# Two units' exponentials in one instruction, under a newly searched order table, in a fused RG-LRU and soft-MoE kernel

## The chip, the cores and the metric

The kernel runs on one core of one Trainium2 chip. The metric is the device time of one execution in microseconds (us). The engines are called PE (TensorE), DVE (VectorE), ACT (ScalarE), POOL (GpSimd) and SP (SyncE, which issues all DMAs of this kernel on one in-order queue).

## The reference

A gated linear recurrence over 4 sequences of 5056 tokens with 256 channels, and a soft mixture of 8 experts with 32 slots over its 20224 outputs. All tensors are float32.

```python
a_base = 1 / (1 + exp(-a_param))
sig_r, sig_i = sigmoid(r_gate), sigmoid(i_gate)
a_t = exp(8 * sig_r * log(clip(a_base, 1e-6, 1 - 1e-6)))
x_gated = sqrt(max(1 - a_t * a_t, 1e-6)) * sig_i * x
for t in range(S):                       # per sequence and channel
    h = a_t[:, t] * h + x_gated[:, t]
    y[:, t] = h
logits = y @ phi                         # 20224 x 32
d = softmax of logits over the tokens
slot_input = d.T @ y                     # 32 slots x 256
slot_out[e] = relu(slot_input[e] @ w1[e]) @ w2[e]
out = softmax of logits over the slots @ slot_out
```

## The kernel before

The tokens are cut into 40 blocks of 512 (the last has 256), numbered 0 to 39. Blocks go in units, mostly of two: 0; 1, 2; 3, 4; 5; 6, 7; 8, 9; and so on to 38, 39. A unit is named by its first block. A block passes through these steps, written with the block's number and, where there are two channel halves, the half:

- r, i and x are loaded (three DMAs of 512 KB). PE transposes r to channels by tokens (rp, L397); ACT takes its sigmoid, or tanh of half of it where the exponential table is active (sr, L409). Per unit, ACT takes the sigmoid of i (si, L420, 128x2048 for two blocks).
- Per unit, ACT computes a = exp(...) (ex), one instruction per channel half, since each half has its own scale. After a sigmoid only a scale is needed (L460), after a tanh a scale and a bias too (L462); both are pointers to a 128x1 column.
- POOL computes a*a (sq, L471) and i*x (u, L432). Per unit, ACT takes sqrt(1 - a*a) (qr, L478).
- PE transposes i*x into PSUM (up, L490). DVE multiplies it with the root (st, L500) and runs the scan (sc, L513), one block and half after the other. PE transposes y back (yp, L533); a copy brings each half block to SBUF (yc), on ACT (L286) or DVE (L288).
- Every four blocks, PE makes logits (lp, L579), DVE takes the running maximum (ls, L589 and L592), PE transposes (ep, L603 and L606), ACT takes exponentials (ee, L612, and md, L597, for the rescaling), PE adds up slots by y (acc, L621), DVE keeps the sum (as, L632).

The functions sigmoid, exp and sqrt sit in different ACT tables, so ACT goes round in stretches: it collects the exponentials and then the roots of about three units and pays an ACT_TABLE_LOAD at each switch. In the plan, copies go with any table and tanh with those of exp and sigmoid.

After the last block come the end of the softmax over tokens (mall, L661; mp, L668; mx; mc, L678; wj; we; W), the slot inputs (sp, L696; slot, L699), the experts on PE (hp, L761; ht, L773; so, L788), and the outputs: logits are transposed per group of four blocks (ct, L841), made to weights (c0, cm, c1, c2, c3, L847 to L861), transposed (hc, L865; hx) and multiplied with the experts' result (op, L894), copied (og, L286 or L288) and stored. Some of ct to c3 run while the experts do.

The order of all of this is written out by hand: ORDER is a table of 1247 numbers, each an operation; a "b" behind a number takes its second engine. The class Plan replays the table with costs to place the tiles: all of r, i, x, a, a*a, weights and outputs live in one tile g (called big in the code) of 19 pairs of 128x2x1024. Each engine, SP too, issues in the table's order. EXM is a list of pairs of units whose exponentials are to be one operation; it is empty before. In e_ex two units are put into one instruction per half when both were made by the same function (plain) and their pairs lie near enough for one strided access pattern; else they follow each other.

Of the kernel before, what the change touches and what calls it, by code (L numbers as in the profile page):

```python
# [13 lines left out]
NEG = -1.0e30  # L14
UNITS = [1] + [2] + [2, 1] + [2] * 17
TANH_I = []
EXM = []
LAST = 3
FIRST = (6, 4)
N_PAIR = 19  # L20
# [6 lines left out]


ORDER = """
# [16 lines left out]
322b 532 864 374 863 375 865 360 320 866 391 393 413 394 395 361 398 362 396 414 379 381 613 417 363 399 397 382  # L46
400 434 454 475 495 435 476 488 507 529 651 711 508 670 467 733 530 489 453 432 380b 472 418 415 419 416 634 632
654 439 436 437 440 868 714 633 635 614 513 715 875 473 477 455 656 438 441 458 456 459 457 460 876 480 478 481
479 877 482 867 869 655 870 871 597 872 873 401 420 736 515 421b 737 402b 556 494 535 514 496 442 499 738 879
497 500 498 739 657 878 880 422 423 501 403 404 443 598 516 536 618 557 577 517 874 537 521 461 463 464 444 881  # L50
518 882 883 540 716 884 445b 599 558 538 519 522 520 752 774 549 548 631 653 692 570 630 589 611 652 671 693 571
590 612 554 462b 717 502 885 523 503 673 483 484 485 486 539 504 505 541 524 886 526 527 887 542 555 562 888 563
559 675 755 560 636 674 595 676 677 757 576 581 695 564 561 525 779 637 596 578 890 756 758 889 780 697 698 891
696 600 565 582 579 583 580 658 617 567 638 777 778 568b 720 679 603 892 893 894 895 566 601 604 602 619 622 543
545 605 544 896 623 546 624 620 621 639 659 640 721 741 680 700 753 793 897 606 796 898 660 641 899 672 694 712
713 608 584 644 607b 585b 625 626b 722 627 586 587b 681 642 645 643 661 646 662 993 795 984 815 794 735 817 663
798 901 664 609 665 775 734 754 965 964 816 970 678 969 776 682 685 908 900 902 761 683 686 684 687 961 699 903
904 905 909 628 910 906 704 718 688 647 648b 689b 666 701 800 797 820 705 907 762 706 702 649 818 650b 821 759
819 690 719 723 740 703 912 668 913 799 911 669b 802 724 667 725 742 707 708 726 709 745 760 782 781 914 915 916
917 767 803 823 801 822 763 727 743 728 746 744 918 747 729 731 764 919 748 920 730 768 765 921 710b 749b 691b  # L60
732b 783 750 786 804 751b 769 766 787 1115 923 805 784 808 924 770 772 925 926 927 928 788 806 785 809 807 810
771b 773b 824 1093 789 791 827 790b 828 825 829 826 930 811 931 813 941 942 932 934 812b 814b 935 943 792 950
967 985 972 981 979 968 989 982 988 971 980 977 978 974 983 966 976 987 975 962 992 973 990 991 986 963 830 945
933 946 922 944 936 951 937 938 939 831 1116 952 953 947 948 929 954 955 956 940 949 1071 1017 957 1039 958 999
1072 1117 1018 994 1073 1000b 995b 1019 959 960 1094 1020 1021 1095 1001 1004 996 997 1040 1009 1118 1005 1002
1074 1075 1010b 1006 1007 998 1011 1003 1096 1119 1012 1097 1041 1042 1043 1008 1013 1022 1098 1044 1076 1120
1045 1014 1015 1016b 1077 1078b 1046 1047 1053 1048b 1050b 1049 1051 1057b 1054b 1099 1055 1100 1059 1056b 1060b
1062b 1063b 1181 1065 1067b 1159 1061 1182 1160 1183 1068b 1069b 1066b 1079 1080b 1081b 1083 1082 1161 1023
1024b 1108 1086 1109 1112 1111b 1110b 1025 1087 1162 1163 1089b 1088b 1090b 1225 1121 1026 1029 1226 1227 1164
1027b 1184 1101 1165 1122b 1028b 1102b 1104b 1032 1103 1105 1166b 1033b 1034 1035 1130 1036b 1131b 1174 1203  # L70
1175b 1177b 1178b 1228 1176b 1133 1134 1132 1185 1186 1204 1205 1229 1230 1123 1124 1127b 1187 1126b 1125 1188
1167 1168 1206 1169b 1171b 1170 1207 1052 1058 1064 1070 1231 1189 1190 1137 1191b 1232b 1193b 1192b 1138 1139
1140 1141 1233 1240 1241 1242 1243 1234b 1235b 1236b 1237b 1244b 1196 1197 1200b 1142 1143 1198 1199b 1208 1209
1144 1152 1153 1156 1154b 1145 1146 1210b 1155b 1218 1219 1222 1147 1148 1220b 1221b 1211 1212 1214 1215b 1149b
1213b 1085 1084 1113 1114 1091 1030 1092 1031 1038 1107 1136 1037 1106 1128 1129 1173 1179 1194 1195 1180 1135
1245 1172 1246 1201 1238 1158 1239 1223 1216 1150 1224 1202 1217 1151 1157
"""


# [11 lines left out]
class Plan:  # L91
# [13 lines left out]
    def op(self, key, eng, us, emit, deps=(), alloc=(), uses=(), act=""):  # L105
        o = Op(key, eng, us, emit, list(deps), list(alloc), list(uses), act)
        assert key not in self.by_key, key
        self.ops.append(o)
        self.by_key[key] = o
# [66 lines left out]
def kernel(  # L176
# [78 lines left out]
    def cols(w):  # L255
        return min(C, NTOK - w * C)


    ident = const.tile([P, P], F32, name="ident")
# [19 lines left out]
    op = plan.op  # L279
# [29 lines left out]
    op(("ident",), "POOL", 0.6, e_ident)  # L309
    op(("ap",), "DMA", 1.7, lambda o: nc.sync.dma_start(out=G(("apl",))[:H, :P], in_=a_param.rearrange("(h p) -> h p", p=P)), alloc=[("G", ("apl",))])  # L310
    op(("yones",), "POOL", 0.3, e_ones)
    op(("misc",), "POOL", 3.2, e_misc)
    op(("phi",), "DMA", 0.2, lambda o: nc.sync.dma_start(out=phi_sb, in_=phi.rearrange("(h p) s -> p h s", p=P)))

    def e_apt(o):
# [41 lines left out]
    def window(w):  # L357
# [80 lines left out]

        exu = [u_ for u_ in units if any(u_[0] in m and u0 in m for m in EXM)] or [unit]
        exk = next((m[-1] for m in EXM if u0 in m), u0)  # L440
        exn = sum(cols(v) for u_ in exu for v in u_) / C
# [524 lines left out]
```

## Time and profile before

| | |
|---|---|
| time, median of 3 runs (range) | 303.35 us (302.66 to 303.78) |
| the profiled execution's own time; its span | 302.85 us; 300.9 us |
| busy: PE, DVE, ACT, POOL | 237.1, 241.3, 241.7, 181.9 us |
| moved by DMA | 100.0 MB: 78.9 read, 20.7 written |
| ACT_TABLE_LOADs | 24 of 1.283 us |

An engine's busy time is averaged over very different stretches. Up to about 27 us blocks are loaded and no scan can run; to about 217 us the blocks pass; to about 246 us PE works on the slots and experts; then the output is written. Which engine has no slack is read per stretch. The span leaves out about 2 us that lie around it in the measured time.

### The profile page before, as it was taken

Reading aid. Unit: us, or ns where it says so; the run is one execution under the profiler, and the core shown is the slowest. Engines: PE = TensorE matmul, PEld = TensorE weight load, DVE = VectorE, ACT = ScalarE, POOL = GpSimd, SP = SyncE. Lnnn points to the kernel's source line nnn. Section 1 sums busy time; section 2 is a strip of 40 time slices with the busy share of each in tenths; the row PEclk is TensorE's granted clock in tenths of the full one; section 3 lists DMA queues with packets and bytes.
Section 4 is the critical chain, followed back from the end, with each engine's and each line's share of the span. In section 5 each row is a group of like instructions: output and inputs, shape, how many; then the busy total and the mean of one; then the engine's idle time right before and its main releaser. Section 6 shows DMA issues by size and latency. Waiting matters only on the chain.

```text
span 300.9 us, 5789 instructions
## 1 busy us (share of the span) xinstructions
PE 237.1 (79%) x2140; PEld 165.0 (55%) x2140; DVE 241.3 (80%) x380; ACT 241.7 (80%) x310; POOL 181.9 (60%) x122
## 2 busy tenths in 40 slices
PE   4606789789896988798898978999899999968500
PEld 4505566565774866557556654757463567655300
DVE  1003999899999999999999999989978759997600
ACT  4999999999999999999999999998223048866400
POOL 4489578995899969799479997895001140022000
PEclk9956999999999999799999999999999999999955
DMA  6999999978998969949997799999990029999997
GB/s 260 380 415 409 400 408 410 401 273 286 413 408 334 411 246 318 378 114 376 412 362 278 256 376 374 344 407 372 332 370 6 2 92 380 403 399 407 377 411 293
DMA packets 28032, 100.03 MB, mean 332 GB/s; under 512 B 3362, under 2 KB 3364, under 8 KB 28004
## 3 DMA queue, kind: packets, MB, share of 16 engines
q1 hardware_dynamic: 28004, 99.66, 86.2%
q8 instruction: 17, 0.28, 0.4%
q14 instruction: 11, 0.09, 0.1%
HBM read 78.94 MB, written 20.71 MB: 331 GB/s over the span
## 4 chain that ended last, share of the span: by engine, by line
PE 28%; DVE 25%; ACT 14%; DMA 10%; issue 8%; POOL 8%; SPq 1%; ACTq 0%; DVEq 0%; POOLq 0%
DVE g L513 11%; DMA g<-in_r_gate_dram 8%; DVE b L500 6%; PE b L894 6%; POOL g L471 4%; ACT g L409 4%; PE b L397 4%; ACT g L462 3%; POOL g L432 3%; PE b L579 3%; PE b L533 3%; PE b L490 2%; PE b L761 2%; DVE y L288 2%; PE b L788 2%
## 5 line engine op out<-in xcount | busy, mean ns | idle before, releaser
L432 POOL TENSOR_TENSOR g<-g 128x1024 f32<-128x1024 f32 (+1 forms) x40 | 93.0, 2345 | 21.6 <-ACT g L420 18.0
L513 DVE TENSOR_TENSOR_SCAN g<-g,b 128x512 f32<-128x512 f32 (+4 forms) x86 | 99.1, 1176 | 0.5
L471 POOL TENSOR_TENSOR g<-g 128x1024 f32<-128x1024 f32 (+1 forms) x40 | 73.8, 1871 | 12.0 <-ACT g L462 8.6
L500 DVE SCALAR_TENSOR_TENSOR b<-g,b 128x512 f32<-128x512 f32 (+1 forms) x80 | 51.7, 676 | 25.7 <-ACT g L478 25.2
L490 PE MATMUL b<-ident,g 128*128 128x128 f32 x316 | 48.3, 285 | 20.9 <-POOL g L432 16.1
L397 PE MATMUL b<-ident,g 128*128 128x128 f32 x316 | 47.7, 292 | 9.0 <-DVE g L513 4.2
L490 PEld LDWEIGHTS b<-ident,g 128*128 128x128 f32 x316 | 35.4, 144 | 33.8 <-POOL g L432 22.4
L533 PE MATMUL b<-ident,g 128*128 128x128 f32 x316 | 46.0, 280 | 6.3 <-DVE g L513 4.5
L397 PEld LDWEIGHTS b<-ident,g 128*128 128x128 f32 x316 | 37.4, 149 | 18.8 <-DVE g L513 7.1
L533 PEld LDWEIGHTS b<-ident,g 128*128 128x128 f32 x316 | 34.3, 141 | 20.5 <-DVE g L513 8.1
L861 POOL TENSOR_TENSOR y<-y,rs 128x512 f32<-128x512 f32 x10 | 10.4, 1048 | 57.9 <-DVE rs L858 40.0
L409 ACT ACTIVATE g<-b 128x512 f32<-128x512 f32 (+1 forms) x80 | 43.1, 605 | 2.1 <-PE b L397 2.1
L288 DVE COPY y<-b 128x512 f32<-128x512 f32 x58 | 38.2, 678 | 1.8 <-PE b L533 1.3
L420 ACT ACTIVATE g<-g 128x2048 f32<-128x2048 f32 (+2 forms) x22 | 38.4, 1755 | 0.1
L478 ACT ACTIVATE g<-g 128x2048 f32<-128x2048 f32 (+2 forms) x22 | 37.3, 1737 | 0.1
L462 ACT ACTIVATE g<-g,ca 128x1024 f32<-128x1024 f32 (+2 forms) x32 | 33.8, 1135 | 0.0
L286 ACT COPY g<-b 128x512 f32<-128x512 f32 (+1 forms) x51 | 24.3, 548 | 10.6 <-PE b L894 10.3
L894 PE MATMUL b<-soR,y 32*128 32x256 f32 x320 | 26.9, 402 | 2.2 <-DVE y L288 0.6
L288 DVE COPY g<-b 128x512 f32<-128x512 f32 (+1 forms) x37 | 22.2, 648 | 3.5 <-PE b L894 3.2
L621 PE MATMUL b<-y,e 128*32 128x257 f32 x316 | 22.4, 385 | 0.6 <-ACT e L612 0.4
L894 PEld LDWEIGHTS b<-soR,y 32*128 32x128 f32 x320 | 18.4, 184 | 7.9 <-ACT g L286 2.6
L286 ACT COPY y<-b 128x512 f32<-128x512 f32 x31 | 17.5, 589 | 6.3 <-PE b L533 6.3
(86 smaller groups left out, 233.8 us busy)
## 6 DMA issues: line engine op xcount, KB each, us to landing
g<-in_x_dram SPq DMA_DIRECT2D x39, 512.0 KB, 7.3
g<-in_i_gate_dram SPq DMA_DIRECT2D x39, 512.0 KB, 7.9
out_dram<-g SPq DMA_DIRECT2D x39, 512.0 KB, 5.7
g<-in_r_gate_dram SPq DMA_DIRECT2D x38, 512.0 KB, 6.5
g<-in_moe_w_dram SPq DMA_DIRECT2D x32, 512.0 KB, 6.2
g<-in_r_gate_dram SPq DMA_DIRECT2D x3, 256.0 KB, 5.5
g<-in_x_dram SPq DMA_DIRECT2D x1, 256.0 KB, 4.6
g<-in_i_gate_dram SPq DMA_DIRECT2D x1, 256.0 KB, 6.4
```

The lines of the kernel that those rows point to most:

```text
L286: nc.scalar.copy(out=dst, in_=srct)
L288: nc.vector.tensor_copy(out=dst, in_=srct)
L397: nc.tensor.transpose(out=by_tile(rp, n)[:, j, :], in_=rows(("r", w), n)[:, j, h * P : (h + 1) * P], identity=ident,)
L409: nc.scalar.activation(halves(("A", w))[:, h, :c], Bk(("rp", w, h))[:, :c], f, scale=k)
L432: nc.gpsimd.tensor_tensor(out=rows(("x", w), n), in0=rows(("i", w), n), in1=rows(("x", w), n), op=ALU.mult)
L462: nc.scalar.activation(a, a, AF.Exp, scale=ca[:, h : h + 1], bias=ca[:, h : h + 1])
L471: nc.gpsimd.tensor_tensor(out=halves(("N", w))[:, :, :c], in0=a, in1=a, op=ALU.mult)
L490: nc.tensor.transpose(out=by_tile(up, n)[:, j, :], in_=rows(("x", w), n)[:, j, h * P : (h + 1) * P], identity=ident,)
L500: nc.vector.scalar_tensor_tensor(up, halves(("N", w))[:, h, :c], 5e-4 if twice else 1e-3, up, op0=ALU.max, op1=ALU.mult)
L513: nc.vector.tensor_tensor_scan(dst, dst, up[:, s0:s1], init, op0=ALU.mult, op1=ALU.add)
L533: nc.tensor.transpose(out=yp[:, j, h * P : (h + 1) * P], in_=halves(("A", w))[:, h, (2 * i + j) * P : (2 * i + j + 1) * P], identity=ident,)
L894: nc.tensor.matmul(Bk(("op",) + tag + (n,))[:, i * D : (i + 1) * D], hT()[r, (2 * i2 + i) * P : (2 * i2 + i + 1) * P], soR[r, :], start=Tr ...
```

## The change

Four pairs of units are named in EXM: 12 and 14, 18 and 20, 30 and 34, 36 and 38. ORDER is another table throughout. The fixed setup operation misc is planned to follow ident.

```diff
-EXM = []
+EXM = [(12, 14), (18, 20), (30, 34), (36, 38)]
 ORDER = """
-1 74 96 5 115 2 0 3 6 7 8 9 10 77 79 101 99 118 78 102 80 100 119 120 83 121 11 16 14 15 33 55 36 58 124 17 60
+5 1 33 55 11 115 74 96 116 34 13 56 12 75 97 138 35 137 57 178 200 76 159 98 219 241 160 179 201 117 0 3 6 7 8 9
...
-    op(("misc",), "POOL", 3.2, e_misc)
+    op(("misc",), "POOL", 3.2, e_misc, deps=[("ident",)])
```

In the built program, the pairs 12 and 14, 30 and 34, 36 and 38 become two instructions of 128x2x2x512 each. Units 18 and 20 stay in four instructions: 18 is made by sigmoid and 20 by tanh in the new order. For unit 38 the new access pattern takes both blocks whole, the last 256 columns of block 39 too, which hold nothing that is read later. ACT has 36 exponentials of blocks instead of 44: 6 of L460 (12 before), 20 of L462 with two blocks (24 before), 4 with one whole block (6 before), none with 256 columns (2 before), and the 6 new ones. Of the 79 copies of y (yc), ACT makes 29 (25 before) and DVE 50 (54 before). There are 24 ACT_TABLE_LOADs before and after, 80 st, 86 scan instructions, and the same DMAs in another order. On DVE, between the first st of unit 30 and that of unit 36, there stand 2 copies of y and 1 as (5 and 2 before); as_7 now stands between the st and the sc of block 38.

On ACT, the exponentials of units 12 and 14, first before, then after. Before, those of 14 (L460) come two sr behind those of 12.

```order
L462 ACT_TABLE_LOAD
L462 ACTIVATE g<-g,ca 128x2x512 x2
L409 ACTIVATE g<-b_76 128x512
L409 ACTIVATE g<-b_70 128x512
L460 ACTIVATE g<-g,ca_91 128x2x512 x2
```

```order
L462 ACT_TABLE_LOAD
L462 ACTIVATE g<-g,ca 128x2x2x512 x2
L409 ACTIVATE g<-b_73 128x512
L597 ACTIVATE d_127<-m_104,n_116 128x1
L612 ACTIVATE e_68<-b_77 128x512
L409 ACTIVATE g<-b_72 128x512
L462 ACTIVATE g<-g,ca 128x2x512 x2
```

Afterwards one double instruction per half covers both, and 14 is among those with a bias. The last row is unit 16.

On ACT, the way to qr_36 and what follows it, before and after. L462 is ex_38 before (with ex_36 and si_38, L420, further ahead), L478 128x2048 is qr_36, L478 128x1024 and 128x2x256 are qr_38, and the L286 are copies of y.

```order
L462 ACTIVATE g<-g,ca 128x512
L462 ACTIVATE g<-g,ca 128x256
L462 ACTIVATE g<-g,ca 128x512
L462 ACTIVATE g<-g,ca 128x256
L478 ACT_TABLE_LOAD
L478 ACTIVATE g<-g 128x2048
L286 COPY y_65<-b_77 128x2x256
L286 COPY y_64<-b_70 128x2x256
L286 COPY y_62<-b_75 128x2x256
L286 COPY y_63<-b_73 128x2x256
L478 ACTIVATE g<-g 128x1024
L478 ACTIVATE g<-g 128x2x256
```

```order
L597 ACTIVATE d_132<-m_109,n_121 128x1
L286 COPY y_66<-b_74 128x2x256
L286 COPY y_63<-b_73 128x2x256
L286 COPY y_62<-b_71 128x2x256
L286 COPY y_66<-b_72 128x2x256
L478 ACT_TABLE_LOAD
L478 ACTIVATE g<-g 128x2048
L478 ACTIVATE g<-g 128x1024
L478 ACTIVATE g<-g 128x2x256
L420 ACT_TABLE_LOAD
L420 ACTIVATE g<-g 128x1024
L420 ACTIVATE g<-g 128x512
```

Afterwards the exponentials of 36 and 38 stand further ahead, in one pair of instructions, four more copies of y stand between qr_30 and qr_36, none stands between qr_36 and qr_38, and si_38 with a table load of its own (the last three rows) has moved behind qr_38.

On PE, from the last copy of y's transposes to the first acc of the last group, before and after: L533 is yp, L603 and L606 are ep_10, L668 is mp, which needs the last maximum of DVE.

```order
L533 MATMUL b_73<-ident,g 128x128 x4
L603 MATMUL b_75<-ident,n_125 128x32
L606 MATMUL b_75<-ident,l_87 128x32
L603 MATMUL b_75<-ident,n_125 128x32
L606 MATMUL b_75<-ident,l_87 128x32
L621 MATMUL b_71<-y_67,e_68 32x257
L621 MATMUL b_71<-y_63,e_68 32x257
L621 MATMUL b_71<-y_64,e_68 32x257
L668 MATMUL b_77<-ident,m_113 1x128
```

```order
L533 MATMUL b_73<-ident,g 128x128 x4
L668 MATMUL b_77<-ident,m_113 1x128
L533 MATMUL b_71<-ident,g 128x128 x4
L603 MATMUL b_74<-ident,n_125 128x32
L606 MATMUL b_74<-ident,l_87 128x32
L603 MATMUL b_74<-ident,n_125 128x32
L606 MATMUL b_74<-ident,l_87 128x32
L621 MATMUL b_73<-y_66,e_69 32x257
```

Before, ep_10 and three acc stand ahead of mp; afterwards mp comes first, and a yp, ep_10 and all of acc_9 and acc_10 stand behind it. Between the last acc and the first hp, PE has three ct, sp and a fourth ct (two ct, sp and a third ct before); the ct that is new there comes from the output part.

More of the change, by code (lines that the diff above doesn't have):

```diff
@@ L29 @@
 ORDER = """
[16 rows of a table removed]
[L46 to L75, printed above, removed]
@@ L76 @@
-1245 1172 1246 1201 1238 1158 1239 1223 1216 1150 1224 1202 1217 1151 1157
[15 rows of a table added]
+507 431 592 508 529 299b 852 530 531 532 611 613 612 614 472 858 509 510 318 354 376 373 355 377 391 411 432 452
+473 392 493 320 337 359 339 319 321 859 374 361 340 360 362 338 465 487 424 464 627 486 446 648 730 415 378 380
+393 412 381 396 860 861 733 653 397 413 398 862 394 416 430 711 587 609 505 527 506 528 451 379b 433 474 470 395
+417 414 492 471 713 630 631 654 712 714 511 864 865 437 456 871 872 438 457 439 453 434 632 478 873 458 435 454
@@ new lines @@
+436 479 455 866 735 867 875 868 475 595 633 736 513 734 876 863 869 418 399 401 459 461 419b 402b 460b 554 476
+480 477 651 420 497 870 400 462 498 421 512 533 516 481 519 483 482 499 494 596 514 534 616 652 874 555 575 515
+597 556 495 484 496 877 878 879 538 880 520 440 441 517 442 535 882 536 518 521 443 539 540 537 881 522 667 500
+883 670 502 668 588 610 628 546 689 568 975 672 649 789 811 547 569 552 553 690 629 650 989 749 770 523b 634 671
+593 541 574 503 884 501 557 560 816 561 543 562 558 544 886 792 542b 673 674 692 576 693 559 594 885 793 887 598
@@ new lines @@
+579 601 635 615 655 752 888 889 890 753 580 602 581 577 603 599 578 775 694 794 620 891 621 600 622 717 776 817
+814 795 695 773 774 815 617 563 565 566 676 618 892 619 604 582 893 584 583 894 524 638 636 656 637 718 738 677
+697 585 895 606 657 641 605b 525b 607b 564b 719 678 660 754 623 897 625 639 658 642 640 710 709 731 669 732 691
+790 812 963 986 965 750 771 969 985 751 772 643 661 659 662 675 715 696 682 679 904 905 626 680 683 906 716 756
+898 755 737 757 701 908 698 681 684 699 702 700 703 723 720 899 900 739 901 902 624b 798 685 686b 663 664b 909
@@ new lines @@
+704 644 705b 665 687 646 896 645b 666b 688b 647b 758 778 759 721 724 722 725 740 799 819 800 742 743 741 903 910
+760 911 706 912 707 744 915 913 763 916 726 745 777 779 782 761 764 762 796 747 917 919 765 780 783 781 784 746b
+727b 748b 766 768 728 1089 767b 920 918 729b 978 977 966 791 971 813 979 962 987 983 968 959 957 797 801 804 921
+818 820 922 923 924 823 805 802 907 769b 914 803 806 974 972 961 824 821 825 822 982 981 958 988 960 967 976 973
+964 980 984 970 785 1067 926 927 786b 807 928 787 937 938 808b 929 788 930 939 946 931 826 827b 940 947 809 810b
@@ new lines @@
+941 932 933 942 948 949 943 934 944 935 1090 950 1068 925 951 945 936 952 1013 1111 1035 953 1177 954 1091 990
+1112 1113 1000 1114 991b 1036 1014 1037 1038 1039 995 992 996 1005 1001 997 1002 993 1069 1015 1070 1115 1016
+1006 1092 998 1071 1017 994 1003 999 1007 1008 1004 1009 1178 1093 1179 1010 955 1116 1040 1018 1094 1072 1041
+956 1011 1073 1042 1074 1180 1012b 1055 1056 1057 1059b 1058b 1043 1049 1044 1047 1050 1053 1046b 1045b 1061
+1095 1052b 1065b 1096b 1062b 1063b 1051 1181 1064 1075 1076b 1077b 1079 1078 1082 1199 1019 1083b 1086b 1084b
@@ new lines @@
+1085 1200 1020 1201 1182 1104 1155 1105b 1107 1156 1097 1157 1133 1108b 1202 1106b 1098b 1099b 1028 1029b 1032b
+1031b 1117 1101 1100 1134 1135 1030 1118b 1021 1022b 1024b 1136 1158 1119 1221 1183 1120b 1184b 1122b 1123b 1025
+1023 1121 1159 1160 1126 1161 1127b 1162b 1129b 1128b 1222 1223 1130 1137 1185 1186 1203 1170 1189b 1187b 1188b
+1138 1192 1171 1174b 1173b 1224 1172b 1193 1204 1196 1139 1163 1140b 1194b 1195b 1148 1164 1167 1165 1225 1149
+1150 1205 1226 1151b 1152b 1166 1206b 1214 1215 1218 1217 1216b 1060 1048 1054 1066 1227 1228b 1141 1207 1208b
@@ L77 @@
+1209b 1210b 1142 1143 1145 1211 1144 1229 1236 1230 1231 1237 1240 1233 1239 1238b 1232b 1080 1081 1087 1088
+1110 1103 1109 1033 1102 1034 1026 1124 1027 1125 1131 1132 1175 1191 1190 1176 1153 1197 1168 1220 1219 1147
+1213 1198 1242 1234 1235 1146 1154 1212 1169 1241
 """
```

29 rows, old and new, of the table ORDER are left out of this document.

## The prediction

> **What bounds the kernel now.** I read the stretches first: the span cut where the first root of units 0, 6, 12, 18, 24, 30 and 36 reaches DVE, then where the experts and the output begin. Columns: stretch, length, busy time of PE, PEld, DVE, ACT, POOL, clock, DMA.
>
> ```profile
> 0.00:26.90 26.90, 9.53 (x57) 8.73 (x58) 0.95 (x6) 22.83 (x30) 17.08 (x38) 0.78 0.92 361
> 26.90:59.20 32.30, 26.33 (x206) 20.52 (x204) 30.07 (x39) 32.21 (x36) 26.41 (x14) 0.97 1.03 406
> ...
> 145.90:175.50 29.60, 26.52 (x228) 17.96 (x224) 28.91 (x44) 29.51 (x30) 23.40 (x12) 1.00 0.86 320
> 175.50:203.00 27.50, 24.37 (x217) 15.52 (x216) 26.14 (x34) 27.38 (x34) 24.41 (x13) 1.00 0.98 377
> 203.00:225.10 22.10, 20.51 (x185) 13.34 (x188) 20.09 (x38) 10.03 (x20) 4.07 (x3) 1.00 0.99 365
> 225.10:246.40 21.30, 21.16 (x255) 10.96 (x254) 15.74 (x43) 6.03 (x13) 5.16 (x5) 1.00 0.02 5
> 246.40:300.90 54.50, 32.27 (x352) 23.06 (x344) 33.54 (x62) 27.27 (x56) 5.19 (x5) 0.85 0.97 381
> ```
>
> From 27 to 203 us ACT never rests and DVE hardly does. At 203 ACT becomes free (10 of 22.1 us) while DVE and PE go on; then PE alone works, then DMA writes. The waits say who leads in the long part:
>
> ```profile
> DVE b L500 <- ACT g L478: 25.2, 5, 22.9
> ACT y L286 <- PE b L533: 6.3, 3, 2.7
> ...
> 173.88 0.72 DVE L589 TENSOR_SCALAR_CACHE_REDUCE l<-b,m 128x512 f32<-128x512 f32 x1
> 175.45 1.29 DVE L500 SCALAR_TENSOR_TENSOR b<-g,b 128x512 f32<-128x512 f32 x2 [0.59 <-ACT g L478]
> 203.01 1.29 DVE L500 SCALAR_TENSOR_TENSOR b<-g,b 128x512 f32<-128x512 f32 x2 [1.30 <-ACT g L478]
> ```
>
> DVE (L500 is st) waits for a root (L478) five times, 22.9 us of it at the start; the other four are 2.3 us together, 1.30 of them for qr_36. ACT waits for transposes of y (L533) three times, and the first row shows that there is no place for that before 203. So ACT paces the blocks through its roots, and DVE, filled up with copies of y, arrives just ahead of each: both are full, but a lighter DVE alone would only wait longer. A saving counts if it brings qr_36 forward and DVE has no more to do before it than ACT; after qr_36, DVE and PE set the end of the blocks, and DMA that of the kernel.
>
> **ACT up to qr_36.** Its rows:
>
> ```profile
> L420 ACT ACTIVATE g<-g 128x2048 f32<-128x2048 f32 x18 | 34.8, 1931 | 0.1
> L462 ACT ACTIVATE g<-g,ca 128x1024 f32<-128x1024 f32 x24 | 28.4, 1252 | 0.0
> L460 ACT ACTIVATE g<-g,ca 128x1024 f32<-128x1024 f32 x12 | 12.9, 1145 | 0.0
> L420 ACT ACT_TABLE_LOAD x7 | 9.0, 1283 | 0.1
> L420 ACT ACTIVATE g<-g 128x1024 f32<-128x1024 f32 x3 | 3.2, 1077 | 0.0
> ...
> 189.40 1.59 ACT L420 ACTIVATE g<-g 128x1024 f32<-128x1024 f32 x2
> 197.24 2.51 ACT L462 ACTIVATE g<-g,ca 128x512 f32<-128x512 f32 x4
> 201.06 1.91 ACT L478 ACTIVATE g<-g 128x2048 f32<-128x2048 f32 x1
> 202.88 2.03 ACT L286 COPY y<-b 128x512 f32<-128x512 f32 x4
> ```
>
> The double exponential is not in the trace. A sigmoid of 2048 takes 1931 - 1077 = 854 ns more than one of 1024; added to 1252 that is 2.11 us, and 2.03 in a row, since 24 of 1252 ns keep ACT busy for 28.4 us, 0.07 less each. Bounds: 1.93 (the sigmoid's, without pointers) and 2.50 (two singles, no saving). I take 2.03, as its nearest row is the same function.
>
> - Exponentials: six L460 (12.9/12 = 1.075 each), four L462 (28.4/24 = 1.18) and unit 38's four (2.51) go, six doubles come: -6.45 - 4.73 - 2.51 + 12.18 = **-1.5 us**. Three units on the dearer form with a bias are in this: of the merging's 2.1, 0.6 is lost.
> - Four copies of y more: the four at 202.88 take 2.03, each after the first (2.03 - 0.59)/3 = 0.48: **+1.9**.
> - si_38 (1.59) and its table load (1.28) move behind qr_36: **-2.9**. One md fewer: -0.2.
>
> Sum: qr_36 ends **2.6 us** earlier (3.2 to -0.2 between the bounds). The same count at the roots before gives +0.3 at 12 and 18, +1.0 at 24, +0.4 at 30: the gain comes in the last stretch alone. Of that stretch's saving, most is not the merging: work is moved out of it, behind a point where ACT rested anyway. DVE must keep up, and there it has three copies of y and one accumulation less, three times 0.6 (the copies' 0.68 less the overlap of a row) and 0.4: 2.2 of 26.1, and its wait of 1.30 goes. From 175.9 (175.45 and ACT's +0.4) it arrives 27.5 - 2.2 - 1.3 = 24.0 later, at 199.9, ahead of the root at 203.0 - 2.6 = 200.4. ACT still decides, with 0.5 us to spare on DVE.
>
> **What the merging delays.** The first unit of a pair gets its exponential only with the second, so its squares on POOL start later.
>
> ```profile
> L471 POOL TENSOR_TENSOR g<-g 128x1024 f32<-128x1024 f32 x39 | 72.8, 1892 | 12.0 <-ACT g L462 8.6 <-issue 2.4 <-ACT g L460 0.7
> ```
>
> A root waits for the two squares of its unit. Between the double exponential of 12 and 14 and qr_12, ACT has eight sr (about 0.5 each), ee, md, the exponentials of 16 and a table load: 8.4 us, against three squares of 1.89 (14's first, then 12's): 2.7 us to spare. For 30 and 34 it is 6.2 against two squares, 3.8; for 36 and 38, eight copies, ee, md and a load, 5.8 against 3.8. So the delay is hidden; uncovered, each square is 1.9 us on ACT's chain, and with it on all that follows.
>
> [...]
>
> **Behind qr_36.** DVE and PE, and what PE does until the first hp:
>
> ```profile
> 212.21 2.44 DVE L513 TENSOR_TENSOR_SCAN g<-g,b 128x512 f32<-128x512 f32 x2
> 215.21 1.38 DVE L513 TENSOR_TENSOR_SCAN g<-g,b 128x256 f32<-128x256 f32 x2
> 219.65 0.15 DVE L661 COPY m<-m 32x1 f32<-32x1 f32 x1
> ...
> 209.71 1.05 PE L621 MATMUL b<-y,e 128*32 128x257 f32 x16
> 219.28 0.24 PE L603 MATMUL b<-ident,n 32*128 32x32 f32 x1
> 219.64 0.63 PE L621 MATMUL b<-y,e 128*32 128x257 f32 x6
> 220.40 1.51 PE L621 MATMUL b<-y,e 128*32 128x257 f32 x18
> 221.84 0.24 PE L678 MATMUL b<-ones,mmax 1*32 1x1 f32 x8
> 222.99 1.23 PE L841 MATMUL b<-ident,l 128*128 128x128 f32 x8
> 224.06 0.53 PE L696 MATMUL b<-Wt,accS 128*128 128x32 f32 x4
> 224.42 0.71 PE L841 MATMUL b<-ident,l 128*128 128x128 f32 x4
> 225.06 3.64 PE L761 MATMUL b<-g,slotT 128*32 128x512 f32 x32
> ```
>
> DVE has the same st and sc, and as_7 (0.45) besides, so mall ends at 219.8 - 2.6 + 0.45 = 217.65. Before, 5.3 us pass from there to hp. After, PE still has mp (0.2), a yp (0.55) and ep_10 (0.35, from 219.28 to 219.64), 28 accumulations of 0.083 (18 in 1.51: 2.3), mc (0.2), three ct (0.6 each: 1.75), sp (0.4) and the fourth ct (0.55), in all 6.3: **+1.0**. hp starts at 223.9, 1.15 earlier. The experts keep their matmuls. PE runs on through that stretch, so each of these counts. The last six of 32 weight loads wait on SP for tiles that the last st free; those come 2 us earlier, and six loads of 512 KB at 399 GB/s (row below) take 7.9 us, until about 222.5; the last one is for the third hp. Were it late, hp would wait for it one to one.
>
> **The output** is one queue:
>
> ```profile
> 216.56 2.02 SPq L739 DMA_DIRECT2D g<-in_moe_w_dram  x4
> 245.74 49.69 SPq L912 DMA_DIRECT2D out_dram<-g  x40
> ...
> 246.00:251.00 5.00, 5.00 (x55) 3.58 (x58) 3.98 (x8) 3.68 (x12) 0.00 (x0) 1.00 0.90 360
> 251.00:253.00 2.00, 1.93 (x32) 1.35 (x28) 2.00 (x4) 1.67 (x4) 0.00 (x0) 1.00 0.79 309
> 253.00:290.00 37.00, 25.74 (x280) 18.43 (x276) 27.88 (x53) 22.28 (x44) 5.19 (x5) 0.93 1.02 399
> ```
>
> DMA is full except at 251 to 253, (1.02 - 0.79) x 2 = 0.4 us. Two ct now stand outside the first products, which come at once: **-0.4**, bounds -0.4 and +1.3 (one store of 512 KB at 399 GB/s late).
>
> **At no cost**, with the cover. misc behind ident: the first r lands later than both; uncovered, under 0.3 us. The start: ACT has the same twelve sr and eight exponentials ahead of si_0, only other units first, and i of block 0 is the 11th block load instead of the 12th, so qr_0 stays where it is; one load more in front of a needed one would be 512 KB at 406 GB/s, 1.3 us, which the roots of 0 to 5 would show and ACT's full row up to 59 would carry on. phi's later load: lp_0 comes long after. POOL, busy 24.4 of 27.5: the squares of 36 to 39 follow each other, then u_37, the clearing of the experts' tile and u_38; that leaves u_38 about 1 us before DVE wants it, beyond which it costs one to one.
>
> **Sum**: -2.6 + 0.45 + 1.0 - 0.4 = -1.55 on the profiled execution's 302.85 (span 300.9 and 1.95 around it): 301.3. The median, 303.35, is 0.5 above it; I predict **301.8 us**.
>
> **Rivals.**
> - *Slower: ACT behind qr_36 becomes the path.* si_38, its table load and four copies of y now stand between qr_36 and ee_8, for which acc_8 and, behind it in PE's queue, the last up, yp and lp wait. From qr_36's end: qr_38 1.6, a load 1.28, si_38 1.59, four copies 1.9, a load 1.28, ee 0.5: ee_8 at 208.6, 8.2 after qr_36 (5.7 before, at 208.8). Then PE has acc_8 (1.05), up, yp and ct (1.6): 211.25, where the scan of block 38 (before, 212.21 and 1.28: 10.5 after the root; now 10.95) lets lp_9 start at 211.35. With 0.2 more before its second half, some 0.3 us of slack. A wait of ACT for transposes, as the three of 6.3 us at its end before, now counts: 301.8 + 6.3 - 0.3 = 307.8 with all, 304.2 with one of 2.7. Beyond 1.85 us (0.3 and the 1.55) the kernel is slower than before. For it: the copies stand close behind DVE's scans. Against: before 203 ACT never waited for a copy.
> - *Faster: PE's added work hides*: before, sp also waited for DVE's sums behind acc_10, and the 0.8 us between the 18 accumulations and 222.99 for four short ones is a wait. If DVE's W sets sp's time after the change too, the +1.0 goes: 300.8; if as_7 also finds a gap of DVE, 300.3. Against: the new order has W done about 0.8 us ahead of sp.
> - *The merging saves nothing*: a strided double costs 2.50. Six times 0.47 comes back: 304.6.
>
> **Chances.** As summed 0.55 (300.9 to 302.9); ACT behind qr_36 0.20; PE's work hides 0.17; no saving 0.08. Half a per cent, 1.5 us, is what a measurement can tell from no change: 301.83 divides the likeliest case in halves. Faster 0.28 + 0.17 = 0.45; same 0.27 + 0.05 + 0.07 = 0.39; slower 0.15 + 0.01 = 0.16. Range: 300.2, at the faster rival's end, to 305.0, past the rival without saving and into ACT's first long wait.
>
> **What the next profile would show.** Six L462 of 128x2048 at about 2.1 us; the wait before DVE's first L500 of unit 36 near 200.4; roots of units 12 to 30 no earlier; ACT busy between 200 and 209; hp near 223.9; DMA without its dip after the first stores. The prediction falls if doubles take 2.4 us or more, if DVE or POOL lag behind ACT in an earlier stretch, or if ACT waits for copies ahead of ee_8.

## The result, and the profile after

The changed kernel takes **302.13 us** in the median (301.2 to 303.94), the kernel before in the same comparison 304.12 us (302.66 to 305.15): ratio 0.9936, 95% interval 0.9918 to 0.9954. It is 0.6% faster, and the interval leaves 1 out. The forecast was 301.8 us (300.2 to 305.0). The profiled execution took 301.67 us (span 299.8) against 302.85 (300.9) before, so the two profiles differ by 1.2 us and the medians by 2.0; run 7, a second profile of before, bears on this.

ACT's groups in the changed kernel, with one line for each shape: the exponentials (L462, L460) and the table loads that now stand at L420.

```profile
L462 ACT ACTIVATE g<-g,ca 128x1024 f32<-128x1024 f32 x20 | 23.9, 1257 | 0.0
L420 ACT ACT_TABLE_LOAD x8 | 10.3, 1283 | 0.1
L462 ACT ACTIVATE g<-g,ca 128x2048 f32<-128x2048 f32 x6 | 12.3, 2099 | 0.0
L460 ACT ACTIVATE g<-g,ca 128x1024 f32<-128x1024 f32 x6 | 6.5, 1140 | 0.0
```

The double takes 2.099 us (2.11 forecast) and 12.3/6 = 2.05 in a row (2.03 forecast). So the second stride of its access pattern adds nothing to the estimate, which came from rows without one.

ACT's timeline at the roots of 6 and 12 before (that of 36, at 201.06, stands in the prediction):

```profile
56.93 5.58 ACT L478 ACTIVATE g<-g 128x2048 f32<-128x2048 f32 x3
87.10 5.62 ACT L478 ACTIVATE g<-g 128x2048 f32<-128x2048 f32 x3
```

After, the same with the root of 36 and with the one wait between 10 and 200 us that was not there before; then DVE ahead of the root of 36, at that root, and at the end of the maximum (mall, L661):

```profile
56.92 5.52 ACT L478 ACTIVATE g<-g 128x2048 f32<-128x2048 f32 x3
67.17 2.56 ACT L409 ACTIVATE g<-b 128x512 f32<-128x512 f32 x5 [0.55 <-PE b L397]
88.29 5.51 ACT L478 ACTIVATE g<-g 128x2048 f32<-128x2048 f32 x3
199.65 3.38 ACT L478 ACTIVATE g<-g 128x2048 f32<-128x2048 f32 x3
...
197.39 0.70 DVE L500 SCALAR_TENSOR_TENSOR b<-g,b 128x512 f32<-128x512 f32 x1 [0.48 <-PE b L490]
201.59 1.29 DVE L500 SCALAR_TENSOR_TENSOR b<-g,b 128x512 f32<-128x512 f32 x2
218.25 0.14 DVE L661 COPY m<-m 32x1 f32<-32x1 f32 x1
```

A first root of a group ends 1.91 or 1.92 us after the row's start. The ends of the roots, and the shift against before:

| root of | before | after | shift | forecast |
|---|---|---|---|---|
| 6 | 58.84 | 58.84 | 0.0 | none given |
| 12 | 89.02 | 90.21 | +1.2 | +0.3 |
| 18 | 118.75 | 119.99 | +1.2 | +0.3 |
| 24 | 145.28 | 147.20 | +1.9 | +1.0 |
| 30 | 175.42 | 176.86 | +1.4 | +0.4 |
| 36 | 202.97 | 201.56 | -1.4 | -2.6 |

So the shape is as forecast (later roots up to 30, the gain in the last stretch alone), but 0.9 to 1.2 us later than forecast throughout, and 0.9 of it is there at the root of 12 already. The wait of DVE for the root of 36, 1.30 before, is gone: DVE and ACT arrive together.

Behind it, PE up to the experts (L761) and the first store:

```profile
218.54 0.27 PE L668 MATMUL b<-ident,m 128*1 128x128 f32 x1
222.09 1.86 PE L841 MATMUL b<-ident,l 128*128 128x128 f32 x12 [0.32 <-DVE accS L632]
223.79 0.53 PE L696 MATMUL b<-Wt,accS 128*128 128x32 f32 x4
224.79 5.36 PE L761 MATMUL b<-g,slotT 128*32 128x512 f32 x48
...
245.07 49.54 SPq L912 DMA_DIRECT2D out_dram<-g  x40
```

mall is 1.40 us earlier (218.25 for 219.65), hp only 0.27 (224.79 for 225.06), the first store 0.67 (245.07 for 245.74). So from hp to the first store it took 20.28 us instead of 20.68. The dip of DMA behind the first stores is filled (share 0.79 before):

```profile
251.00:253.00 2.00, 2.00 (x31) 1.54 (x24) 2.00 (x4) 1.37 (x3) 0.00 (x0) 1.00 1.02 391
```

### The profile page after: what moved, and what is told of

The parts are those of the page before. It is cut to its first block, busy times and chain, and to the rows that moved or that the text cites. A ratio compares the mean times of both kernels' runs of the same rounds, so it can differ in the third digit from the quotient of the medians.

```text
span 299.8 us, 5788 instructions
## 1 busy us (share of the span) xinstructions
PE 234.7 (78%) x2140; PEld 166.0 (55%) x2140; DVE 239.7 (80%) x379; ACT 242.2 (81%) x303; POOL 181.9 (61%) x122
## 4 chain that ended last, share of the span: by engine, by line
ACT 28%; PE 27%; POOL 15%; issue 12%; DVE 7%; DMA 4%; DVEq 0%; POOLq 0%; ACTq 0%
POOL g L471 8%; POOL g L432 5%; ACT g L462 4%; ACT g L420 4%; ACT g L478 4%; PE b L397 4%; ACT y L286 4%; ACT g L409 4%; PE b L894 4%; DMA g<-in_x_dram 4%; PE b L533 3%; PE b L490 3%; DVE g L288 3%; PE b L788 2%; PE b L761 2%
## 5 line engine op out<-in xcount | busy, mean ns | idle before, releaser
L490 PE MATMUL b<-ident,g 128*128 128x128 f32 x316 | 48.5, 289 | 22.0 <-POOL g L432 20.2
L490 PEld LDWEIGHTS b<-ident,g 128*128 128x128 f32 x316 | 36.3, 146 | 35.0 <-POOL g L432 23.6
L397 PE MATMUL b<-ident,g 128*128 128x128 f32 x316 | 46.7, 293 | 6.0 <-DMA g<-in_r_gate_dram 3.7
L533 PE MATMUL b<-ident,g 128*128 128x128 f32 x316 | 44.7, 284 | 8.3 <-DVE g L513 6.8
L397 PEld LDWEIGHTS b<-ident,g 128*128 128x128 f32 x316 | 37.9, 151 | 15.7 <-issue 4.2
L533 PEld LDWEIGHTS b<-ident,g 128*128 128x128 f32 x316 | 35.8, 144 | 18.8 <-DVE g L513 11.2
L409 ACT ACTIVATE g<-b 128x512 f32<-128x512 f32 (+1 forms) x80 | 42.4, 604 | 2.9 <-PE b L397 2.9
L462 ACT ACTIVATE g<-g,ca 128x1024 f32<-128x1024 f32 (+2 forms) x30 | 39.1, 1371 | 0.0
L420 ACT ACTIVATE g<-g 128x2048 f32<-128x2048 f32 (+2 forms) x22 | 37.9, 1744 | 0.1
L478 ACT ACTIVATE g<-g 128x2048 f32<-128x2048 f32 (+2 forms) x22 | 36.8, 1732 | 0.1
L288 DVE COPY y<-b 128x512 f32<-128x512 f32 x53 | 34.6, 680 | 2.1 <-PE b L533 1.5
L286 ACT COPY g<-b 128x512 f32<-128x512 f32 (+1 forms) x45 | 22.2, 567 | 8.7 <-PE b L894 8.0
L288 DVE COPY g<-b 128x512 f32<-128x512 f32 (+1 forms) x43 | 24.7, 629 | 2.5 <-ACT y L286 0.8
L286 ACT COPY y<-b 128x512 f32<-128x512 f32 x36 | 20.0, 601 | 5.7 <-PE b L533 4.4
L579 PE MATMUL b<-g,phi_sb 128*32 128x512 f32 (+1 forms) x160 | 22.4, 622 | 0.0
```

Source lines behind the costliest of these rows:

```text
L286: nc.scalar.copy(out=dst, in_=srct)
L288: nc.vector.tensor_copy(out=dst, in_=srct)
L397: nc.tensor.transpose(out=by_tile(rp, n)[:, j, :], in_=rows(("r", w), n)[:, j, h * P : (h + 1) * P], identity=ident,)
L409: nc.scalar.activation(halves(("A", w))[:, h, :c], Bk(("rp", w, h))[:, :c], f, scale=k)
L420: nc.scalar.activation(a, a, AF.Tanh if twice else AF.Sigmoid, scale=0.5 if twice else 1.0)
L462: nc.scalar.activation(a, a, AF.Exp, scale=ca[:, h : h + 1], bias=ca[:, h : h + 1])
```

## The experiments

**1. The merging taken out of the new order.** `e_ex` never puts two units in one instruction; the table of numbers is the same.

```diff
-                if plain(exu[0]) == plain(exu[1]) and ...
+                if False and plain(exu[0]) == plain(exu[1]) and ...
```

> The changed kernel with its order untouched, but the three double exponentials taken apart again. A pair of singles per half costs 2 x 1.195 where the double costs 2.05 in a row, so ACT gets 0.68 us more ahead of qr_12, 0.68 ahead of qr_30 and 0.80 ahead of qr_36. My theory (ACT's chain up to qr_36 sets the time, and DVE behind it is full): qr_36 2.2 us later than in the changed kernel (203.7), the time 304.3 us, so the whole gain is gone and the ratio to the kernel before is 1.000. Rival (the gain is the new order's, and POOL's earlier squares or DVE's slack absorb the rest): 302.1 us, ratio 0.994.

Measured 303.66 us, ratio 0.998 (0.9962 to 0.9998). The root of 12 came 0.70 later than in the changed kernel, that of 30 1.25, that of 36 1.92 (203.48), and the first store 1.91: what is put on ACT ahead of qr_36 arrives undiminished at the output. In the medians it is 1.5 us; by the ratios to the kernel before, 0.998 here against 0.9936 and, in run 10, 0.9949, it is 1.3 or 0.9 us. The rival that the merging is worth nothing falls.

**2. The merging alone, in the old order.** Two pairs that already stand next to each other on ACT are put into doubles.

```diff
-EXM = []
+EXM, JOIN = [], {28: 24, 34: 32}
-            parts_ = [[u_] for u_ in exu]
+            parts_ = [] if u0 in JOIN.values() else [[unit, unit_of[JOIN[u0]]]] if u0 in JOIN else [[u_] for u_ in exu]
```

> The kernel before, its order untouched, with two pairs of exponentials that already stand next to each other on ACT (28 and 24, 34 and 32) put into doubles. Rival (merging pays by itself, 0.68 us a pair): the root of 24 0.7 earlier, that of 36 1.4 earlier, 302.8 us, ratio 0.9955. My theory (the merging delays the squares of the first unit by about 1.0 us each time, and POOL is busy without a gap there, so part of it comes back as a wait of ACT for a later root): the roots of 24 and 30 0.7 earlier, but then waits of up to 0.8 us at the roots of 26 and 32; the root of 36 0 to 0.7 earlier, 303.4 to 304.1 us, ratio 0.998 to 1.000.

Measured 304.80 us, ratio 1.0023 (0.9999 to 1.0046): nothing won, and the interval does not show a loss. ACT's timeline has the two waits (at the roots of 26 and 32), and PE's the one that follows from them, since POOL's products come late too:

```profile
148.83 1.91 ACT L478 ACTIVATE g<-g 128x2048 f32<-128x2048 f32 x1 [0.64 <-POOL g L471]
180.59 1.91 ACT L478 ACTIVATE g<-g 128x2048 f32<-128x2048 f32 x1 [0.60 <-POOL g L471]
...
182.93 1.09 PE L490 MATMUL b<-ident,g 128*128 128x128 f32 x8 [1.81 <-POOL g L432]
```

From the root of 18 to that of 24 the doubles saved 0.55 us (25.98 for 26.53), but from 30 to 36 the kernel lost 1.58 (29.13 for 27.55), with PE at half clock from 184 to 187, behind that wait. Here doubles did not pay, as the squares behind them were late; in the new order no root waited for squares.

**3. si_38 put back ahead of qr_36, in the new order.** The order by names:

```diff
 si_36
+si_38
 ...
 qr_38
-si_38
```

> The changed kernel with si_38 alone moved back ahead of qr_36, beside si_36; the table load that it needed behind qr_38 goes. My theory: qr_36 1.6 us later (203.1), and all of it on DVE's path: 303.7 us, ratio 0.9985, although ee_8 comes 1.3 us earlier (207.9). Rival (ACT's chain of si_38, load and copies behind qr_36 and PE's queue behind acc_8 set the end): no later than 302.1, down to 300.8.

Measured 303.22 us, ratio 0.9968 (0.9947 to 0.9989): 1.1 us of the gain gone in the medians (1.0 or 0.6 by the ratios of the changed kernel, 0.9936 and 0.9949). From the root of 30 to that of 36 it took 26.15 us for 24.70, 1.45 of the expected 1.6 (in its profile another 1.4 had been lost by the root of 30, most of it beside a half clock that lasted from 152 to 159). What was wrong is ee_8: it came 7.3 us after the root, not 4.8 (7.6 in the changed kernel). Without si_38 and its load ACT simply waits there for transposes of y:

```profile
207.04 1.08 ACT L286 COPY y<-b 128x512 f32<-128x512 f32 x2 [1.16 <-PE b L533]
208.35 0.58 ACT L286 COPY y<-b 128x512 f32<-128x512 f32 x1 [0.23 <-PE b L533]
209.81 0.59 ACT L286 COPY y<-b 128x512 f32<-128x512 f32 x1 [0.87 <-PE b L533]
```

These are 2.26 us of rest, into which si_38 and its load had been moved. The forecast's rival of ACT behind qr_36 falls with it.

**4. The same move alone, in the old order.** qr_38, si_38 and POOL's products of 38 and 39 stand directly behind ls_8, ahead of the copies of y.

```diff
-si_38   (ahead of si_36)
 qr_36
 ...
 ls_8
+qr_38
+si_38
```

> The kernel before with one thing of the change alone: si_38, and with it the products of 38 and 39 on POOL, moved behind qr_38; ACT pays one table load more there. My theory: qr_36 1.6 us earlier (201.4), DVE then 0.3 late for it (201.7), so the end of the blocks and the time 1.3 us earlier: 302.8 us, ratio 0.9957, two thirds of the gain without any merging. Rival (si_38 behind qr_38 makes u_38, or ee_8 and PE's queue, late, and only the whole new order can place it there): 304.1 us or more.

Measured 306.47 us, ratio 1.0063 (1.004 to 1.0086): slower, as the rival said, by a mechanism that neither named. From the root of 30 to that of 36 it took 26.50 us for 27.55, so 1.05 of the expected 1.6 did arrive there; behind the root the kernel lost more, as mall came 19.97 us after it instead of 16.68. In the old order the copies of y come after qr_36; held up behind si_38 they keep their PSUM banks, and PE, then DVE, stand:

```profile
208.56 0.66 PE L490 MATMUL b<-ident,g 128*128 128x128 f32 x4 [1.93 <-ACT y L286]
...
209.35 1.29 DVE L500 SCALAR_TENSOR_TENSOR b<-g,b 128x512 f32<-128x512 f32 x2 [1.07 <-PE b L490]
212.66 0.70 DVE L500 SCALAR_TENSOR_TENSOR b<-g,b 128x512 f32<-128x512 f32 x1 [0.83 <-PE b L490]
```

With two later waits for PE, of 0.53 and 0.56, these make 3.0 of the 3.3 us; a spell of PE's half clock, from 209.4 to 212.8, is in them. The new order makes four copies ahead of qr_36 (the +1.9 of the forecast); by this reading that is the price that makes the move possible, which no run tests alone.

**5. Where much of the lateness arose: PE's clock.** In the changed kernel PE stands twice for POOL's products, and in the stretches behind them the profile shows a lower clock (third column from the right):

```profile
62.67 1.11 PE L490 MATMUL b<-ident,g 128*128 128x128 f32 x4 [2.27 <-POOL g L432]
96.17 1.43 PE L490 MATMUL b<-ident,g 128*128 128x128 f32 x8 [2.68 <-POOL g L432]
...
62.00:64.00 2.00, 1.33 (x6) 1.33 (x7) 2.00 (x4) 1.97 (x3) 2.00 (x2) 0.66 0.99 373
64.00:66.00 2.00, 2.00 (x11) 2.00 (x11) 2.00 (x4) 2.00 (x2) 1.20 (x2) 0.50 1.02 410
66.00:68.00 2.00, 2.00 (x19) 1.89 (x18) 2.00 (x3) 1.45 (x4) 2.00 (x1) 0.99 1.01 408
96.00:98.00 2.00, 1.83 (x11) 1.83 (x12) 2.00 (x3) 2.00 (x2) 0.11 (x1) 0.69 1.01 410
98.00:100.00 2.00, 2.00 (x12) 2.00 (x11) 1.75 (x4) 2.00 (x2) 1.09 (x1) 0.50 1.03 422
100.00:102.00 2.00, 2.00 (x19) 1.95 (x18) 2.00 (x4) 1.96 (x4) 2.00 (x2) 0.95 1.02 414
```

Twelve transposes of r at 63.58 take 2.69 us there, where twelve at 66.54, at full clock, take 1.47; ACT's wait of 0.55 at 67.17 is for them. The test fills both waits with transposes of the identity into banks that are written later.

```diff
                 up = Bk(("up", w, h))
+                for j in WARM.get((w, h), []):      # block 8: 16, block 14: 20
+                    nc.tensor.transpose(out=banks[WB[w]][:, j * P : (j + 1) * P], in_=ident, identity=ident)
```

> The changed kernel, its order untouched, with throwaway transposes of the identity on PE at the two places where PE stood waiting for POOL's products: 16 ahead of the first transpose of i*x of block 8 (a wait of 2.27 us at 60.4 in the changed kernel) and 20 ahead of that of block 14 (2.68 us at 93.5). They write to banks that are overwritten later; the result is unchanged. My theory (each of these waits is followed by about 3.5 us in which the profile shows PE at half its clock, r's transposes come late, and ACT's roots of 12 with them: this is why they came 1.2 later than before instead of the 0.3 forecast): no half clock at 62 to 66 and at 96 to 101, ACT's wait of 0.55 at 67.17 gone, the root of 12 0.5 to 0.6 earlier (89.65), the time 301.6 us if DVE keeps up. Rival (the half clock comes by itself, or is due to how much PE has worked, not to the wait): the low clock stays at these places and the time at 302.1 us. Second rival (DVE, full there, takes the gain away): the clock is full, the root 0.5 earlier, the time 302.1 us.

Measured 301.22 us, ratio 0.9924 (0.9907 to 0.9942). The clock stays full at both places, ACT's wait is gone, and from the root of 6 to that of 12 it takes 30.72 us instead of 31.37:

```profile
60.59 1.97 PE L488 MATMUL b<-ident 128*128 128x128 f32 x16
62.95 0.66 PE L490 MATMUL b<-ident,g 128*128 128x128 f32 x4 [0.39 <-POOL g L432]
63.44 1.57 PE L397 MATMUL b<-ident,g 128*128 128x128 f32 x12
...
62.00:64.00 2.00, 1.61 (x16) 1.37 (x14) 2.00 (x4) 1.98 (x2) 2.00 (x2) 1.00 0.91 350
64.00:66.00 2.00, 1.92 (x17) 1.51 (x15) 2.00 (x4) 1.99 (x2) 1.22 (x1) 1.00 0.99 391
```

So the half clock goes when the wait is filled, although PE then works more, and useless work on an engine that is not the bound made the kernel faster (301.22 us for 302.13 in the medians). One rival is left open by this run: within a profile the spells of half clock begin at multiples of 3.41 us from one another, on a grid that lay otherwise in another execution (last section), and in run 5, with a spell from 153.08 on, it lay 1.7 us later than in the changed kernel's profile. Run 8 settles it: its grid (a spell from 182.72 on, so a place at 63.25) lay between those of runs 3 and 1, in whose profiles both spells stand (from 63.1 and 97.2, and from 63.6 and 97.7), and with the waits filled it has neither.

**6. The same waits filled with real work.** Two transposes of r (15, 12) go ahead of block 8's first product, block 12's transposes of y ahead of block 14's.

```diff
+rp_15_0 rp_12_1
 up_8_1
-rp_15_0 rp_12_1
 ...
+yp_12_0 yp_12_1
 up_14_1
-yp_12_0 yp_12_1
```

> The changed kernel with two real pieces of work moved into the same waits of PE: two transposes of r (of 15 and 12) ahead of the first product of block 8, and block 12's two transposes of y ahead of the first product of block 14. Each fills 1.2 us, so the waits shrink to about 1.1 and 1.5 us. My theory: the half clock goes or is shorter, the root of 12 0.5 to 0.9 earlier, 301.3 to 301.7 us. Rival (a wait of 1.1 us is enough for the half clock): the clock falls as before, the root of 12 0 to 0.5 earlier, 301.8 to 302.1 us.

Measured 301.57 us, ratio 0.993 (0.9912 to 0.9947). At 62 the clock stays full with a wait of 1.26 us left; at 98 it falls once more, behind waits of 0.94 and 1.34, which fall into one period of that grid. The root of 12 ends at 89.63, 0.6 earlier.

**7. A second profile of before.** Nothing is changed.

> The kernel before once more, for a second profile of it. Both other kernels with its order (and no change ahead of 130 us) showed the root of 6 0.9 and 1.2 us later than the profile that the forecast was made from (57.9 and 58.1 where that one started it at 56.9), with a longer stretch of half PE clock at 28 to 32 us. If that is the usual run, this profile has the root of 6 start near 58, and the changed order's start is worth about 1 us that the forecast, made on a lucky profile, could not see; if not, it starts near 56.9.

Its run took 305.53 us, more than any of the 11 other runs of this kernel beside it (302.66 to 304.53). The root of 6 starts at 57.87, as expected, and that of 36 ends at 204.94 instead of 202.97. A second microsecond is lost at the root of 16, where ACT waits for squares, since POOL started late on the product of 13, since that block's x came late:

```profile
79.27 2.38 POOL L432 TENSOR_TENSOR g<-g 128x1024 f32<-128x1024 f32 x1 [2.18 <-DVE b L500]
92.79 1.91 ACT L478 ACTIVATE g<-g 128x2048 f32<-128x2048 f32 x1 [1.01 <-POOL g L471]
...
g<-in_x_dram SPq DMA_DIRECT2D x1, 512.0 KB, 5.5
```

(The last row is that transfer: issued at 73.56, landed 5.5 us later; in the first profile issued at 72.62, landed after 4.5, and the product started at 77.30. DVE, which the first row names, had long been done.) The forecast was made from a profile that had escaped both losses. But this one is no usual execution either: of the 87 runs of the kernel before in five comparisons, two were shorter than the first profile's 302.85 and three longer than 305.53, and the medians lie from 303.71 to 304.15.

**8. Three waits filled.** As 5, with 24 transposes more ahead of block 24's transposes of y, where PE waits 3.2 us.

```diff
+WARM: block 24, first transposes of y: 24
```

> The changed kernel with throwaway transposes at three places: the two of the run with two (16 ahead of block 8's first product, 20 ahead of block 14's) and 24 ahead of the transposes of y of block 24, where PE waits 3.2 us for DVE at 148.4 and runs at half clock from 153. Theory: that half clock goes too; ACT waited for nothing behind it in the run with two, so the usual run gains nothing, only the runs in which the low clock lasts for two periods (as one profile showed, where ACT lost 0.7 and DVE 1.8 us): 301.2 us, ratio 0.992 to before. Rival (DVE, late by hundredths at the root of 30, gains from earlier transposes of y): 300.8 us.

Measured 301.80 us, ratio 0.9932 (0.9919 to 0.9945): no better than two, as expected. The low clock at 153 is gone; in its profile there was one at 183 to 186 instead, and the root of 36 ended at 201.76, where that of run 5 ended at 201.02, though their roots of 30 ended 0.02 apart.

**9. The kernel before with its waits filled.** 96 throwaway transposes ahead of block 0's first product, 16 ahead of block 14's.

```diff
+WARM: block 0: 96, block 14: 16
```

> The kernel before, its order untouched, with throwaway transposes at the two places where its second profile was slower than its first: 96 ahead of block 0's first product (PE waits 12 us there and then runs at half clock until 31) and 16 ahead of block 14's (a wait of 1.96 us, half clock at 95 to 98). Theory (the first profile was one in which both happened to cost nothing; about 1 us is lost at each in the usual run): the root of 6 starts at 56.9 and that of 36 ends near 203.0, 302.0 to 302.8 us, ratio 0.994 to 0.997, so that at equal clocks the change itself is worth about 1.2 us and not the 2.0 of the medians. Rival (the start is late for another reason, its loads): 303.7 us.

Measured 305.82 us, ratio 1.0058 (1.0042 to 1.0074): slower, against both theories. The half clock at the start was not removed but moved, to the stretch from 26.5 to 33.3; the 96 were done at 23.8, and PE stood 1.92 and 0.94 us after them. At 95 it was gone, but x of 13 landed 6.2 us after its issue, and ACT waited 1.71 us for squares at the root of 16. What the old order lost there in this run is the transfer's, not the clock's.

**10. The changed kernel once more.**

> The changed kernel once more, beside the two others: 302.1 us, ratio 0.9936 to before, and the profile again with half clock at 62 to 66 and 96 to 101, since the waits of PE that lead to it stand in its order.

Measured 302.35 us, ratio 0.9949 (0.9935 to 0.9962). The half clock stood at the same places (0.66, 0.50 and 0.69, 0.50), and the roots of 12 and 18 ended at 90.21 and 120.01, within 0.02 of the first profile. The new order repeats itself where the old one's two profiles differ by 2 us, though in both of its profiles the grid of the half clock happened to lie at the same place (a spell from 62.64 on).

**11. An order searched on.** A new table of numbers, made as the expectation says.

```diff
 ORDER = """
-5 1 33 55 11 115 74 96 116 34 13 56 12 75 97 138 ...
+(another order from si_0 on)
```

> The changed kernel under an order that was moved on from its own in small steps, by a plan whose durations on ACT, DVE and POOL are those measured in the changed kernel's profile, with a price on every wait of PE above 1.2 us between 30 and 243 us; no throwaway work. In that plan the six such waits of the changed order (2.4 us at 60, 2.7 at 93, 1.8 at 123, 3.3 at 148, 1.2 at 162, 2.3 at 179) are gone. Theory (PE's waits, through its half clock, are what is left to gain ahead of the root of 36): no half clock between 31 and 243 or one spell at most, the root of 36 0.6 to 1.5 us earlier than in the changed kernel (200.1 to 201.0), 300.6 to 301.4 us, ratio 0.989 to 0.992. Rival (a plan without the chip's transfers and clock opens other waits, as moving si_38 in the order before did): 302.1 us or more.

Measured 306.79 us, ratio 1.0087 (1.0056 to 1.0119). The half clock was gone from 34 to 243, as meant, and the kernel was slower by more than 4 us in the medians (3.1 in the profiles): a load of i now came late (and with it 1.52 us of ACT), DVE waited for products, and the root of 36 ended at 202.70, 1.1 late. From the first st of 36 to mall it then took 18.6 us for 16.66, with a second accumulation of slots and a first reduction for the output on DVE in between, and the first store came 2.8 later:

```profile
129.67 1.92 ACT L420 ACTIVATE g<-g 128x2048 f32<-128x2048 f32 x1 [1.52 <-DMA g<-in_i_gate_dram]
135.80 1.99 DVE L500 SCALAR_TENSOR_TENSOR b<-g,b 128x512 f32<-128x512 f32 x3 [1.20 <-PE b L490]
...
247.87 49.76 SPq L912 DMA_DIRECT2D out_dram<-g  x40
```

**12. Two waits filled, again.**

> The changed kernel with throwaway transposes at two places once more, beside the searched order: 301.2 us, ratio 0.9925; half clock neither at 62 to 66 nor at 96 to 101.

Measured 301.41 us, ratio 0.9922 (0.99 to 0.9944). With run 5 it is the fastest version, in both at 0.992 of before, where the changed kernel is at 0.994 and 0.995. The intervals overlap; what tells the two apart is the profiles (30.72 and 30.74 us from the root of 6 to that of 12, for 31.37).

## Why the prediction was right, and where it was wrong

- *The doubles* (2.03 in a row): 2.05. Run 1 shows that they are worth what they take off ACT, 1.9 us in the profile.
- *ACT up to qr_36* (-2.6): -1.41. This is the mis-sized term. By stretches, forecast and measured: to the root of 12 +0.3 and +1.2; 12 to 18 0.0 and 0.05; 18 to 24 +0.7 and +0.7; 24 to 30 -0.6 and -0.5; 30 to 36 -3.0 and -2.85. Counting instructions was right; what failed is that the forecast took it that no new wait of ACT arises in an earlier stretch. 0.6 of it is the half clock at 62 to 66, shown by run 5, which gives 0.64 back. 0.26 is the start, where ACT waited 2.36 us for the first transposes of r (2.10 before); that was not tested.
- *DVE half a microsecond ahead*: no. It needed 24.57 us from its first st of 30 to that of 36, not 24.0, and came with the root: it waited 0.48 us for a product of PE (the row at 197.39) and 0.13 for a copy, which the forecast had at nothing.
- *as_7* (+0.45): nothing. From st_36 to mall it took 16.66 us, 16.64 before; as_7 (0.4) is made up for behind the last scan, from whose start to the end of mall it took 3.55 us for 3.93: a copy of y now stands ahead of the last maximum and not behind it.
- *PE between mall and hp* (+1.0): +1.13, and so the rival that this work hides falls. hp at 224.79 instead of 223.9, because mall came 1.40 earlier and not 2.15. PE is busy 22.4 of the 23.2 us from 201.6 to 224.8.
- *The output* (-0.4): right, 0.79 to 1.02 of DMA at 251 to 253; from the first store to the end it took 0.47 less. But the 0.40 between hp and the first store stands in no term: the forecast kept that stretch as it was. The same matmuls of the experts stand there in another order, and why that is shorter was not tested.
- *ACT behind qr_36* (rival): its chain was as long as worked out (ee_8 ended 8.2 after the root), and lp_9 started 1.0 us later than its scan allowed, but DVE took its result without a wait. Run 3 shows that ACT had 2.3 us of rest there.
- *The sum.* The terms sum to -1.55, the profiles differ by 1.18. That this is near is in part luck: ACT fell short by 1.2 and PE by 0.1, and as_7 (0.45) and the stretch from hp to the first store (0.40) made up for most of it.
- *The median.* The forecast set the median 0.5 above the profile, from three runs; the changed kernel's lies 0.46 above its own, so 302.13 is the 0.3 or 0.4 that the terms were too hopeful. The old kernel's median of 16 runs lies 1.27 above its profile, which was one of its shortest executions (run 7), and so the medians differ by 2.0. One part of this is the start: the root of 6 ended at 58.84 in that profile, but at 59.78, 59.79 and 60.03 in the three others with the old order and no extra work (runs 7, 2 and 4), and between 58.8 and 59.1 in all eight with the new order (the changed kernel, runs 1, 3, 5, 6, 8, 10 and 12). No term of the forecast held that. The new order is not steadier as a whole: its times spread over 2.7 us, those of the old one over 2.5.

What stays open: why the old order's start is late in most of its profiles. The half clock of the start ended at 28.6 us in the early one and at 30.2, 30.4 and 31.9 in the three late ones; with the new order an end at 30.2 (run 5) did not make the root late, and run 9 did not part the clock from the loads.

## What to carry to other kernels

Put work into one longer instruction where its engine sets the pace and what waits for its first half has time to spare; merging gave 0.9 to 1.5 us in one order and nothing in another. Where the tensor engine is not the bound, look in the profile for its waits of about 2 us (2.27 and 2.68 here) and for a clock below 1 behind them (0.50 here): filling such a wait, even with useless work, can pay more than what it costs (0.64 us up to the root of 12 in run 5), if the engine that sets the pace waits for what PE does next; a third wait filled gained nothing (run 8). Take a second profile of the kernel before you sum against the first, since one profile can miss waits that other runs have, and see from the times of many runs where each of the two lies.

## What the runs showed of the hardware

- Between 34 and 198 us the rows of 2 us of the 14 profiles show PE's half clock in spells of 3.4 us (23 of them), once of twice that. A spell of t us lowers the mean clock of a 2 us row by t/4, so the rows of the changed kernel shown with run 5 give 1.36 + 2.00 + 0.04 = 3.40 us from 62.64 on, and 1.24 + 2.00 + 0.20 = 3.44 from 96.76 on; in run 3 one lasted 6.84. Within a run the spells stand on one grid: in the changed kernel 96.76 and 127.48 lie 10 and 19 times 3.41 behind 62.64. On that grid, standing for 1.95 us of the period ahead (1.73 and 0.22, from 124.1 on) was followed by a spell; in run 5, where the grid lay otherwise (a spell from 153.08 on), the same wait of 1.73 fell alone into a period and was not. In the first profile of the kernel before and that of the changed kernel the grids have 138 periods at full clock from 31 to 275 us. In four of them PE stood, without a matmul or a weight load, for 1.91 to 2.68 us, and each of the four was followed by half clock in the next; in the other 134 it stood for 1.74 us at most, and none was.
- Where the grid lies differed from one execution to another: a spell began at 62.64 in the changed kernel, at 63.1 in run 3 and at 63.6 in run 1, of the same order up to there. In the changed kernel waits of 2.27 and 2.68 us were each followed by a spell.
- So two executions of one program can differ in which waits are followed by a spell: in the kernel before, spells began at 124.1 in the first profile, and at 95.0 and 125.8 in the second. What a spell costs differs too: that at 62.64 cost 0.64 us, and from the root of 12 to that of 18, with that at 96.76, it took 29.79 us for 29.63 in run 5.
- A load of 512 KB landed 4.5, 5.5 and 6.2 us after its issue, the same load (x of block 13) in three runs of one order (the first profile of the kernel before, runs 7 and 9), with a DMA share of 0.93 meanwhile in the first.
